# Ordering a one-core forward and backward kernel: from a greedy planner in program order to a planner by latest times with free accumulator banks

## The chip, the core and the metric

The kernel runs on one core of one Trainium2 chip. The time is device microseconds of one execution, and a kernel is judged by the median of its runs. Engines are named as the profile names them: PE (TensorE matmul) with PEld (its weight loads), DVE (VectorE), ACT (ScalarE), POOL (GpSimd), SP (SyncE). ACTq, SPq and POOLq are the queues on which these engines issue transfers.

## What is computed

The reference is a layer and its gradients. With x of 2048 rows by 512 columns:

```python
xn = layernorm(x)                               # no affine part
K  = Re( sum_n C[d,n] * exp(dt[d]*A[d,n]*l) * dt[d]*B[d,n] )   # 512 kernels of length 2048, n = 128 complex states
s  = causal_convolution(xn, K) + xn * Dskip     # the reference does it by FFTs of length 4096
g  = silu( silu(xn @ w1) @ w2 )                 # 512 -> 1792 -> 512
out = x + s * g
```

The outputs are `out` and the gradients, for a given `grad_out`, of x, the six parameter arrays of A, B and C (512 x 128 each), log_dt, Dskip, w1 and w2: twelve outputs, all bf16.

## The kernel before

Row l of x is stored as l = 16 p + t: partition p (128 of them) and t from 0 to 15. The convolution is done on four blocks of 128 channels (b = 0 to 3). Each transform is two steps of matmuls with a set of transposes between them: `dft_fwd` (tiles dA, dB; accumulators ps_s1, pt_f, ps_s2) and `dft_inv` (ps_i2, ps_i1); `cplx_mul` on DVE multiplies the spectra (tiles sp_in, cm2). The profile shortens names that end in a digit: ps_s, ps_i, ps_w.

The recorded stages are:

- Setup: x is loaded in four pieces and normalized (xn); parameters are loaded transposed by DMA (`load_params`, L609); 31 exponentials make the magnitudes (mag_all, L635); sine tables (TF, L416), small constants.
- Tables and forward (`chain`, paced with `gen_ffn_fwd` at 0.58 steps): per block `gen_tables` makes powers of the state matrix (sine on ACT, products E and Y on DVE) and, by matmuls ps_k and ps_e, the kernel KE, which goes through a DRAM tensor Kd to be read back as Kb; `gen_conv_x` transforms xn; `gen_conv_fwd` transforms Kb, multiplies and inverts. `gen_ffn_fwd` runs the two feed-forward matmuls in eight chunks of 256 rows (ps_h, hT, Silu to aT, ps_o, ob) and stores hT to Hd and ob to Od.
- Gates: `gen_gate_rows` applies Silu (g, L864) and its derivative (L873) to the feed-forward rows and forms ds and do, beside the last block's forward convolution.
- Backward convolution (`gen_conv_bwd`) beside `gen_ffn_da`, which reads Hd back (dhT), takes the derivative, multiplies by ps_da, stores DHd, and accumulates ps_dx; `gen_out` writes the forward result.
- Gradients of the state parameters (`gen_ssm_bwd`): it loads the parameters again, folds the gradient of K (GE from dKd, accumulator G, Gf), multiplies with transposed Y tables (YT, ps_v, Vb), with E (Tp) and sums on PE (psS). It runs beside the rest of `gen_ffn_da`.
- Weight gradients: `gen_dw2` (h_in transposed to a_tok, ps_w2) and `gen_dw1` (dh_tok by DMA transposes from DHd, ps_w1), then the layer norm backward `gen_ln_bwd`.

Accumulator memory has eight banks in three pools: `pf` (three tiles of one bank; feed-forward, PE transposes and weight gradients), `pc` (two tiles of two banks; transforms, ps_v, G) and `pt` (one tile of one bank; tables, psS). Evacuations go through the helper `Evac`, so L295 (ACT) and L296 (DVE) are the line of nearly all copies out of accumulators.

What sets the order is a planner at the end of the kernel. The program is written with generators that are woven by hand-set rates (`woven`, `paced`, `interleave`); that gives the recorded order. The class `Plan` then reads the recorded instructions, works out for each the instructions it must follow, and `solve` simulates the engines: every engine, SP's and POOL's queue too, takes whenever it is free the ready instruction that comes first in the recorded order. Costs come from formulas in `cost`: a matmul takes its columns at 2.4 per ns (twice that in stretches its clock model calls cold), an ACT instruction 78 ns + 0.82 per element, a change of activation table 1283 ns more; a transfer has an issue time on its queue, then 900 ns, then its packets on one shared line, then 1200 ns until a reader may start. `apply` ties each engine's instructions together in the planned order with dependencies that need no semaphore.

Two of its rules matter here:

```python
before[t.name] = first[same[-1]] if same and str(t.space) != "DRAM" else None
if len(same) >= bufs and str(t.space) != "DRAM":
    old[t.name] = users[same[-bufs]]
...
heapq.heappush(ready[eng[n]], n)
```

A tile of a tag may not start before the tile recorded ahead of it, and it waits for the users of the tile `bufs` places earlier: tiles take their buffers in turn. This holds for accumulator tiles as for others. The last line is the priority: the number n in the recorded order.

Of the kernel before, what the change touches and what calls it, by code (L numbers as in the profile page):

```python
# [18 lines left out]
P = 128  # L19
# [14 lines left out]

class Plan:
# [3 lines left out]
    SEM, ROOM = 80.0, 212863  # L39

    def __init__(self, nc, tc):
        self.tc, self.ins, self.deps, self.starts = tc, [], [], []
        cells, users, first, tags, pools, before, old, placed = {}, {}, {}, {}, {}, {}, {}, []
# [3 lines left out]
        for x in nc.cur_bb.bb.instructions:  # L47
# [16 lines left out]
            n, eng, dep = len(self.ins), x.engine.name, set()  # L64
# [4 lines left out]
            for ap, writes in [(a, False) for a in ins] + [(a, True) for a in outs]:  # L69
                t = ap.tensor  # L70
                tag = getattr(t, "tag", None)
                if tag is None:
                    if not writes:
                        continue
                elif t.name not in users:
                    same = tags.setdefault(tag, [])
                    bufs = t.tag_meta.bufs
                    before[t.name] = first[same[-1]] if same and str(t.space) != "DRAM" else None
                    if len(same) >= bufs and str(t.space) != "DRAM":
                        old[t.name] = users[same[-bufs]]  # L80
                    same.append(t.name)
                    first[t.name], users[t.name] = n, set()
                if tag is not None:
                    dep |= old.get(t.name, set())
                    if before[t.name] is not None and before[t.name] != n:
                        self.starts.append((before[t.name], n))
                    users[t.name].add(n)
                    pools.setdefault(int(tag.rsplit("_", 1)[1]), set()).add(n)
                q, idx, size = self.cells(ap)
                last, readers = cells.setdefault(t.name, (np.full(size, -1, np.int32), {}))  # L90
                spots.append((writes, q, idx, last, readers))
                for k in q:
                    for r in [last] + (list(readers.values()) if writes else []):
                        dep.update(np.unique(r[k, idx]).tolist())
            for writes, q, idx, last, readers in spots:
                for k in q:
                    if writes:
                        last[k, idx] = n
                        for r in readers.values():
                            r[k, idx] = -1  # L100
                    else:
                        readers.setdefault(eng, np.full(last.shape, -1, np.int32))[k, idx] = n
            self.deps.append(dep - {-1, n})
        for i, (a, a0, a1) in enumerate(placed):
            for b, b0, b1 in placed[i + 1:]:
                if a0 < b1 and b0 < a1 and a in pools and b in pools:
                    self.starts.append((pools[a], pools[b]))

    @staticmethod
    def cells(ap):  # L110
# [14 lines left out]
        for s, n in sorted(dims, key=lambda d: -d[0]):  # L125
            if s and n > 1:
                step = np.append(np.arange(0, n, g), n - 1) if s == 1 else np.arange(n) * s
                idx = (idx[:, None] + step).ravel()
                if s < g:
                    idx = np.unique(idx // g) * g  # L130
# [9 lines left out]
    def cost(self, x):  # L140
# [44 lines left out]
    def solve(self):  # L185

        N = len(self.ins)
        succ, wait = [[] for _ in range(N)], [len(d) for d in self.deps]
        for n, d in enumerate(self.deps):
            for m in d:  # L190
                succ[m].append(n)
        begun = [[] for _ in range(N)]
        groups = []
        for a, b in self.starts:
            if isinstance(a, int):
                begun[a].append(b)
                wait[b] += 1
            else:
                groups.append([len(a), b])
                for m in a:  # L200
                    begun[m].append(-len(groups))
                for m in b:
                    wait[m] += 1
        cost = [self.cost(x) for x in self.ins]
        eng = [x.engine.name for x in self.ins]
        dma = ["DMA" in type(x).__name__ or "Dma" in type(x).__name__ for x in self.ins]
        ready = {e: [] for e in set(eng)}
        free = dict.fromkeys(ready, 0.0)
        line, tables = 0.0, "nesd"
        heat, warm = {}, {0: False}  # L210
        self.plan = {e: [] for e in ready}
        events, self.start = [], [0.0] * N
        for n in range(N):
            if not wait[n]:
                events.append((0.0, 1, n))
        heapq.heapify(events)
        when = [0.0] * N
        end = 0.0

        def met(m, t):  # L220
            wait[m] -= 1
            when[m] = max(when[m], t)
            if not wait[m]:
                heapq.heappush(events, (when[m], 1, m))

        def clock(t):
# [3 lines left out]
            return warm[w]  # L230
        while events:
            t, kind, n = heapq.heappop(events)
            if kind == 1:
                heapq.heappush(ready[eng[n]], n)
                e = eng[n]
            else:
                e = n
            while ready[e] and free[e] <= t:
                n = heapq.heappop(ready[e])
# [6 lines left out]
                elif e == "Activation" and not dma[n]:  # L246
                    f = self.SETS.get(getattr(self.ins[n], "func", None))
                    if f:
                        both = "".join(c for c in f if c in tables)
                        if not both:  # L250
                            d, l = d + 1283.0, l + 1283.0
                        tables = both or f[0]
                self.plan[e].append(n)
                self.start[n] = t
                free[e] = t + d
                heapq.heappush(events, (free[e], 2, e))
                if dma[n]:
                    line = max(line, t + (d if e == "Pool" else min(d, 330.0)) + 900.0) + l
                    done = line + 1200.0
                else:  # L260
                    done = t + l + self.SEM
                end = max(end, done)
                for m in succ[n]:
                    met(m, t + d if e == "PE" == eng[m] else done)
                for m in begun[n]:
                    if m >= 0:
                        met(m, t)
                    else:
                        g = groups[-m - 1]
                        g[0] -= 1  # L270
                        if not g[0]:
                            for y in g[1]:
                                met(y, t)
        assert sum(map(len, self.plan.values())) == N, "the plan is not complete"
        return end

    def apply(self):

        edge = mybir.DependencyInfo(mybir.DependencyClass.NoSync, mybir.DependencyReason.DATA)
        for line in self.plan.values():  # L280
            for a, b in zip(line, line[1:]):
                self.tc.add_manual_dep(self.ins[b], self.ins[a].name, edge, reason="plan")
# [90 lines left out]
def turned_in_place(k, W, ev):  # L373

    blocks = W[:].rearrange("p a (b n) -> p (a b) n", n=P)
    turned(k, lambda i: blocks[:, i], blocks.shape[1], blocks, ev)
# [285 lines left out]
def gen_tables(k, b):  # L662
# [69 lines left out]
    bc = lambda ap, n: ap.unsqueeze(2).to_broadcast([P, ap.shape[1], n, 32])  # L732
# [4 lines left out]
    ev(KE[:, 1:8, 0:2, :], bc(A[:, 0:7], 2))  # L737
# [10 lines left out]
    ev(KE[:, 2:4, 3:6, :], bc(B[:, 3:5], 3))  # L748
    ev(KE[:, 2:8, 6:8, :], bc(B[:, 6:12], 2))
# [48 lines left out]
def gen_ffn_fwd(k):  # L798
    nc, fp = k.nc, k.fp
    D, FT, DK, T = k.D, k.FT, k.DK, k.T  # L800
    for c in range(T // 2):
# [21 lines left out]
        if c == T // 2 - 1:  # L823
            turned_in_place(k, k.W1, k.evw)
# [467 lines left out]
@with_exitstack  # L1292
def kernel(ctx, tc, A_u, A_A_re, A_A_im, A_B_re, A_B_im, A_C_re, A_C_im, A_log_dt, A_Dskip, B_x, B_w1, B_w2, grad_out,
           out_0, out_1, out_2, out_3, out_4, out_5, out_6, out_7, out_8, out_9, out_10, out_11):
    nc = tc.nc
    k = KCtx()
    k.nc, k.tc = nc, tc
    k.outs = [out_0, out_1, out_2, out_3, out_4, out_5, out_6, out_7, out_8, out_9, out_10, out_11]
    L, D, F = A_u.shape[1], A_u.shape[2], B_w1.shape[1]
# [5 lines left out]
    k.x_v, k.g_v, k.o0_v, k.o1_v = tl(A_u[0]), tl(grad_out[0]), tl(out_0[0]), tl(out_1[0])  # L1305

    def pool(name, side=None, es=ctx, **kw):
        kw.setdefault("bufs", 1)
        return es.enter_context(tc.tile_pool(name=name, side=side, reuse_waits="tile", **kw))
    dr = ctx.enter_context(tc.tile_pool(name="dram", bufs=1, space=DRAM))  # L1310
# [16 lines left out]
    k.pf = ctx.enter_context(tc.tile_pool(name="pf", bufs=3, space=PSUM))  # L1327
    k.pc = ctx.enter_context(tc.tile_pool(name="pc", bufs=2, space=PSUM))
    k.pt = ctx.enter_context(tc.tile_pool(name="pt", bufs=1, space=PSUM))
# [87 lines left out]
    turned_in_place(k, k.W2, k.evw)  # L1417
# [18 lines left out]
    plan = Plan(nc, tc)  # L1436
    plan.solve()
    plan.apply()
# [28 lines left out]
```

## Time and profile before

| | |
|---|---|
| median of three runs | 699.57 us (696.84 to 700.85) |
| profiled execution: span, first to last instruction | 694.4 us |
| profiled execution: its own total time | not given beside the span; the median above is 5.2 us more |
| instructions | 15206 |
| mean granted clock of PE | 0.950 |
| DMA | 148.85 MB, mean 214 GB/s |
| chain that ended last, by engine | PE 48%, ACT 20%, DVE 13%, DMA 9%, issue 4%, SPq 4%, ACTq 2% |
| activation table loads | nine of 1.28 us, five of them in the gates |

Busy time of an engine is the time in which one of its instructions runs; PE's overlaps PEld's. In a row for a stretch the columns are length, busy time and count of PE, PEld, DVE, ACT and POOL, then granted clock (1.00 is full), share of the 16 DMA engines and GB/s. A row of waits reads: who, its tile and line, the one waited for; total us, times, longest. A row of a timeline reads: start, duration, engine or queue, line, operation, output <- input, count.

### The profile page before, as it was taken

To read this page: it belongs to the slowest core of one execution; us is meant where nothing else is said; L and a number is where in the kernel's file an instruction comes from. 1 tells how busy PE (TensorE), PEld (TensorE's weight loads), DVE (VectorE), ACT (ScalarE), POOL (GpSimd) and SP (SyncE) were. 2 spreads that over 40 slices of the span, in tenths; PEclk is the share of its full clock that TensorE was granted. 3 is DMA by queue.
4 is the path that set the end of the run, shared out by engine and by line. 5 is a ranking of instruction groups with operands and counts; after the bars stand their busy time and mean duration, and the time that the engine had idled before them with its cause. 6 is when DMAs were issued, how large, how long until landed. Compare 5 with 4: busy or idle time off the path is not lost.

```text
span 694.4 us, 15206 instructions
## 1 busy us (share of the span) xinstructions
PE 573.5 (83%) x6268; PEld 416.6 (60%) x6268; DVE 521.0 (75%) x917; ACT 470.8 (68%) x630; POOL 79.9 (12%) x163
## 2 busy tenths in 40 slices
PE   0599697878979785469998998928998879999988
PEld 0455564547657564256765756626966656865877
DVE  6959987979989585869797979415798533966971
ACT  6959765978887988997867775406648438744541
POOL 1274100010001000000000000000002020023211
PEclk9989998999999998779999999978999999999999
DMA  9864536584557487968886775594899996747994
GB/s 297 331 145 154 196 142 225 206 274 168 189 192 260 178 292 259 287 227 274 263 273 204 236 228 176 144 236 116 168 215 221 223 252 147 172 124 243 261 253 124
DMA packets 158773, 148.85 MB, mean 214 GB/s; under 512 B 79280, under 2 KB 136112, under 8 KB 155120
## 3 DMA queue, kind: packets, MB, share of 16 engines
q1 hardware_dynamic: 145664, 125.07, 63.0%
q0 software_dynamic: 6144, 17.83, 7.1%
q10 hardware_dynamic: 6896, 4.98, 2.3%
q8 instruction: 49, 0.80, 0.5%
q14 instruction: 20, 0.16, 0.1%
HBM read 65.14 MB, written 64.36 MB: 187 GB/s over the span
## 4 chain that ended last, share of the span: by engine, by line
PE 48%; ACT 20%; DVE 13%; DMA 9%; issue 4%; SPq 4%; ACTq 2%; DVEq 0%
PE ps_w L1234 6%; PE ps_o L829 6%; PE ps_dx L1184 5%; PE ps_w L1216 5%; PE ps_da L1173 4%; ACT dA L295 4%; PE ps_h L812 2%; ACT mag_all L635 2%; PE psS L1032 2%; PE ps_i L573 2%; ACT sn L684 2%; PE pt_t L362 2%; PE ps_v L1010 2%; PE ps_i L582 2%; PE psS L1036 2%
## 5 line engine op out<-in xcount | busy, mean ns | idle before, releaser
L295 ACT CAST dA<-ps_s 128x1024 bf16<-128x1024 f32 x96 | 94.0, 1032 | 14.5 <-PE ps_s L541 9.9
L829 PE MATMUL ps_o<-W,aT 128*128 128x512 bf16 x224 | 62.8, 417 | 11.9 <-ACT hT L295 11.6
L812 PE MATMUL ps_h<-XT,W 128*128 128x256 bf16 x448 | 60.3, 279 | 6.5 <-DVE XT L296 5.0
L1173 PE MATMUL ps_da<-doT,W 128*128 128x256 bf16 x448 | 60.9, 276 | 3.1 <-ACT doT L295 1.8
L1020 DVE TENSOR_TENSOR Tp<-Vb,Eb 128x1344 bf16<-128x1344 bf16 x64 | 52.6, 855 | 10.2 <-ACT Vb L295 7.8
L1175 DVE TENSOR_TENSOR dhT<-ps_da,dhT 128x512 bf16<-128x512 f32 x56 | 37.7, 686 | 28.7 <-PE ps_da L1173 28.5
L295 ACT CAST dB<-ps_i 128x1024 bf16<-128x1024 f32 x48 | 47.0, 1027 | 17.3 <-PE ps_i L573 14.2
L295 ACT CAST Vb<-ps_v 128x672 bf16<-128x672 f32 x64 | 44.0, 740 | 18.8 <-PE ps_v L1010 15.2
L1184 PE MATMUL ps_dx<-W,dhT 128*128 128x512 bf16 x224 | 55.5, 380 | 0.0
L1216 PE MATMUL ps_w<-YD,a_tok 128*128 128x512 bf16 x224 | 53.4, 379 | 0.5 <-ACT a_tok L1201 0.5
L812 PEld LDWEIGHTS <-W 128*128 128x128 bf16 x448 | 42.4, 100 | 18.4 <-issue 10.9
L295 ACT CAST o<-ps_w 128x256 bf16<-128x256 f32 (+1 forms) x42 | 18.7, 445 | 50.0 <-PE ps_w L1234 28.1
L1234 PE MATMUL ps_w<-dh_tok,xn 128*128 128x256 bf16 x448 | 49.4, 273 | 3.1 <-DMA dh_tok<-DHd 3.1
L1173 PEld LDWEIGHTS <-W 128*128 128x128 bf16 x448 | 41.3, 99 | 13.4 <-issue 6.2
L1234 PEld LDWEIGHTS <-xn 128*128 128x128 bf16 x448 | 43.7, 98 | 8.9 <-DMA dh_tok<-DHd 2.1
L829 PEld LDWEIGHTS <-aT 128*128 128x128 bf16 x224 | 21.2, 105 | 37.9 <-issue 17.9
L573 PE MATMUL ps_i<-I,sp_in 64*128 64x128 bf16 x768 | 32.5, 229 | 11.6 <-DVE sp_in L596 8.7
L573 PEld LDWEIGHTS <-sp_in 64*128 64x128 bf16 x768 | 23.8, 99 | 24.5 <-DVE sp_in L596 12.3
L295 ACT CAST hT<-ps_h 128x512 bf16<-128x512 f32 x56 | 32.1, 617 | 8.1 <-PE ps_h L812 4.9
L296 DVE COPY dB<-pt_f 128x2048 bf16<-128x2048 bf16 x24 | 28.3, 1218 | 11.4 <-PE pt_f L547 11.4
L557 PE MATMUL ps_s<-dB,F 128*64 128x512 bf16 x192 | 29.5, 389 | 7.1 <-ACT dA L295 5.3
L295 ACT CAST pd_s<-ps_dx 128x512 bf16<-128x512 f32 x16 | 9.4, 590 | 35.7 <-DMA Pd<-pd_s 17.0
(222 smaller groups left out, 1301.9 us busy)
## 6 DMA issues: line engine op xcount, KB each, us to landing
Yd<-YD SPq DMA_DIRECT2D x8, 1024.0 KB, 5.3
sp_in<-Ud SPq DMA_DIRECT2D x8, 1024.0 KB, 8.1
h_in<-Hd SPq DMA_DIRECT2D x14, 512.0 KB, 4.8
Ed<-E SPq DMA_DIRECT2D x8, 672.0 KB, 4.0
Eb<-Ed SPq DMA_DIRECT2D x8, 672.0 KB, 5.6
Hd<-hT POOLq DMA_DIRECT2D x8, 512.0 KB, 5.8
Ud<-dA SPq DMA_DIRECT2D x4, 1024.0 KB, 4.8
KXd<-dA SPq DMA_DIRECT2D x4, 1024.0 KB, 6.0
```

The costliest lines, as they stand in the source:

```text
L295: return self.nc.scalar.copy(out=out, in_=in_)
L296: return self.nc.vector.tensor_copy(out=out, in_=in_)
L557: nc.tensor.matmul(out=ps[64 * h:64 * h + 64, 4 * v:4 * v + 4], lhsT=k.F2[:, c, :], rhs=Bv[:, u, v, h], start=True, stop=True)
L573: nc.tensor.matmul(out=ps[:, h, g], lhsT=Y[hs, c, 4 * q + g, :], rhs=k.I2[hs, c].rearrange("p c m -> p (c m)"), start=(c == 0), stop=(c == 1))
L812: nc.tensor.matmul(out=ps[:, j], lhsT=k.W1[:, dk, ft * P:ft * P + P], rhs=XTv[:, :, dk, :], start=(dk == 0), stop=(dk == DK - 1))
L829: nc.tensor.matmul(out=ps[:], lhsT=aT[:, ft, t * P:t * P + P], rhs=k.W2[:, ft, :], start=(ft == 0), stop=(ft == FT - 1))
L1020: k.nc.vector.tensor_tensor(out=Tp[:, c, :, r ^ c].rearrange("p e (q w) a -> p q w e a", w=2), in0=Vb[:, :, c].rearrange("p q w (e a) -> p ...
L1173: nc.tensor.matmul(out=ps[:, j], lhsT=k.W2[:, ft, dk * P:dk * P + P], rhs=dTv[:, :, dk, :], start=(dk == 0), stop=(dk == DK - 1))
L1175: nc.vector.tensor_tensor(out=dh[:, i0:i0 + 2, :], in0=ps[:], in1=dh[:, i0:i0 + 2, :], op=ALU.mult)
L1184: nc.tensor.matmul(out=ps[:], lhsT=dhs[ft // 8][:, ft % 8, t * P:t * P + P], rhs=k.W1[:, :, ft * P:ft * P + P], start=(ft == 0), stop=(ft ...
L1216: nc.tensor.matmul(out=ps[:], lhsT=at[:, t, :], rhs=k.do[:, t, :], start=(t == 0), stop=(t == k.T - 1))
L1234: nc.tensor.matmul(out=ps[:], lhsT=k.xn[:, t, dk * P:dk * P + P], rhs=dh[:, t].rearrange("p j n -> p (j n)"), start=(t == 0), stop=(t == k ...
```

## The change

The kernel's body becomes a function `body` that is called with a `Recorder` in the place of the engines. The recorder notes each operation with its arguments; `Room` and `Later` stand for pools and tiles, `View` for a slice of one. The noted program is then written twice by `emit`: once, in the recorded order, into a draft program from which `Plan` reads instructions and dependencies, and once into the real program, in the planner's order and with the planner's places for accumulator tiles. `tie` (formerly `apply`) ties each engine's line as before.

The planner changes in these ways:

- Accumulator tiles no longer take their buffers in turn. Each bank (or pair, in `pc`) is a place of its own; a tile takes any vacant place of its pool when its first instruction starts. The last vacant place is kept for the tile of that pool that is oldest in recorded order. Tiles in SBUF still go in turn.
- `backward` runs the plan from the end and gives every instruction the latest time at which it could start. `forward` takes, on each engine, the ready instruction with the earliest latest time, not the first recorded. The two alternate for up to eight rounds, for six settings, and the plan with the shortest modelled end is kept.
- A transfer isn't issued earlier than `hold` (30, 40 or 55 us) before its latest time.
- When the next ACT instruction would change the activation table, another that doesn't is taken first if its due time lies within `table` (3 or 8 us).
- Readers of a piece of a tile are all kept for the dependencies of the next writer, where before only the last reader of each engine was.

The costs are the same. The core of the diff:

```diff
 class Plan:
-    SEM, ROOM = 80.0, 212863
+    SEM, ROOM, LAND = 80.0, 212863, 1200.0
+    TRIES = [(hold, table) for hold in (4e4, 3e4, 5.5e4) for table in (3000.0, 8000.0)]
+    ROUNDS = 8
...
+        for (tag, bufs, space), names in tags.items():
+            lists = [list(users[t]) for t in names]
+            if space == "PSUM":
+                self.homes[tag] = bufs
+                for title, u in zip(names, lists):
+                    for n in u:
+                        self.uses[n].append(len(self.tiles))
+                    self.tiles.append((tag, u))
+                    self.titles.append(title)
+                continue
+            for a, b in zip(lists, lists[1:]):
+                if a[0] != b[0]:
+                    self.order.append(([a[0]], [b[0]]))
+            for a, b in zip(lists, lists[bufs:]):
+                for n in b:
+                    self.pred[n].update(m for m in a if m != n)
...
-    def solve(self):
+    def forward(self, key, latest=None, hold=0.0, table=0.0):
...
+        def release(n, t):
+            push(events, (max(t, latest[n] - hold) if latest and dma[n] else t, 1, n))
...
+        def full(i):
+            h = tiles[i][0]
+            q = queue[h]
+            while q and q[-1] in prior:
+                q.pop()
+            return not vacant[h] or (len(vacant[h]) == 1 and q[-1] != i)
...
-                heapq.heappush(ready[eng[n]], n)
+                push(ready[e], (key[n], n))
...
+                shut = [i for i in homeless(n) if full(i)]
+                if shut:
+                    blocked[tiles[shut[0]][0]].append(n)
+                    continue
+                if e == "Activation" and loads(n):
+                    aside, other = [], None
+                    while ready[e] and ready[e][0][0] < k + table and other is None:
...
+                for i in homeless(n):
+                    h = tiles[i][0]
+                    prior[i], slot[i] = vacant[h].pop(0)
+                    wake(h, t)
...
+    def backward(self, p):
...
+                for m in pred[n]:
+                    lag = self.LAND if dma[m] else cost[m][0] if e == "PE" == eng[m] else cost[m][1] + self.SEM
+                    need[m] = max(need[m], back[n] + lag)
...
+    def solve(self):
+
+        self.best = None
+        first = self.forward(range(self.N))
+        for hold, table in self.TRIES:
+            p = first
+            for _ in range(self.ROUNDS):
+                back = self.backward(p)
+                length = max(back)
+                p = self.forward([length - b for b in back], [p.end - b for b in back], hold, table)
+                if self.best is None or p.end < self.best.end:
+                    self.best = p
+        return self.best.end
+
+    def places(self):
+        return {self.titles[i]: ("%s_%d" % (self.tiles[i][0].rsplit("_", 2)[0], y), 1) for i, y in self.best.slot.items()}
...
+def tile_recurrent_scan__ssm_conv_s4__dense_activation_silu__prompt_kernel(ctx, tc, *args):
+    rec = Recorder()
+    ports = [View(None, None) for _ in args]
+    L, D, F = args[0].shape[1], args[0].shape[2], args[10].shape[1]
+    with ExitStack() as es:
+        body(es, rec, L, D, F, *ports)
...
+    ins, made = rec.emit(dtc, zip(ports, copies))
+    plan = Plan(draft, dtc)
     plan.solve()
-    plan.apply()
+    slots = {t.name: s for s, t in made.items() if isinstance(s, Later)}
+    order = plan.best.sequence
+    done, _ = rec.emit(tc, zip(ports, args), order, {slots[t]: home for t, home in plan.places().items()})
+    plan.tie(tc, dict(zip(order, done)))
```

More of the change, by code (lines that the diff above doesn't have):

```diff
@@ L233, in solve @@
+        loads = lambda n: self.func[n] and not dma[n] and not any(c in tables for c in self.func[n])
+        homeless = lambda n: [i for i in uses[n] if i not in prior]
+        for n in range(N):
+            if not wait[n]:
+                release(n, 0.0)
+        while events:
+            t, kind, n = pop(events)
+            if kind == 0:
+                vacate(n, t)
+                continue
+            e = n
             if kind == 1:
-                heapq.heappush(ready[eng[n]], n)
```

410 lines of the change are left out of this document (290 added, 120 removed).

## The prediction

> **What bounds the kernel now.** I read the page's busy line first, then its stretches by stage, then who waited for whom, and last the SyncE queue in the one stretch that stands still. The first two lines show busy time and granted clock.
>
> ```profile
> PE 573.5 (83%) x6268; PEld 416.6 (60%) x6268; DVE 521.0 (75%) x917; ACT 470.8 (68%) x630; POOL 79.9 (12%) x163
> ...
> PEclk9989998999999998779999999978999999999999
> ```
>
> No engine is full. Whether TensorE's 573.5 us is real work I check by rates: 32 matmuls of 512 columns in one unbroken run take 6.91 us (0.216 each), 128 of 256 columns 14.13 us (0.110), 32 transposes of 128 columns 1.79 us (0.056). 672 x 0.216 + 1344 x 0.110 + 2350 x 0.056 is 425 us; the narrow ones at their own rows' rates (L557 0.155, L573 0.039, L718 0.048, L1010 0.093, others 10 in all) add 119. So about 540 us of the 573.5 is work, and a perfect order of this work could not go below some 560 (540, plus the 20 before the first matmul). That is a floor, not a forecast.
>
> The second view is the span in stages:
>
> ```profile
> 0.00:20.00 20.00, 0.00 (x0) 0.00 (x0) 14.76 (x43) 14.27 (x26) 4.01 (x49) 1.00 0.95 297
> 20.00:104.00 84.00, 69.73 (x637) 48.79 (x638) 72.99 (x135) 64.74 (x89) 26.01 (x31) 0.94 0.55 190
> 104.00:260.00 156.00, 130.54 (x1567) 90.42 (x1566) 134.64 (x184) 125.65 (x178) 11.55 (x14) 0.97 0.62 220
> 260.00:312.00 52.00, 29.43 (x343) 23.43 (x341) 34.48 (x50) 48.63 (x49) 0.56 (x1) 0.77 0.80 258
> 312.00:441.00 129.00, 123.91 (x1511) 84.55 (x1509) 111.01 (x154) 91.36 (x102) 6.48 (x12) 0.99 0.72 229
> 441.00:471.00 30.00, 15.37 (x113) 10.48 (x111) 7.34 (x13) 6.04 (x6) 0.00 (x0) 0.84 0.84 211
> 471.00:590.00 119.00, 107.19 (x1177) 83.04 (x1174) 75.97 (x149) 71.73 (x102) 10.69 (x20) 0.95 0.89 192
> 590.00:660.00 70.00, 69.20 (x679) 51.33 (x680) 55.78 (x162) 37.87 (x62) 15.39 (x28) 1.00 0.73 199
> 660.00:694.40 34.40, 28.14 (x255) 24.51 (x253) 13.99 (x31) 10.56 (x23) 5.17 (x8) 0.99 0.79 189
> ```
>
> After the length stand busy PE, weight loads, DVE, ACT and POOL, then clock, DMA share and GB/s. The reader is to see different limits: to 260 DVE leads at 207.6 of 240 with nothing full; from 260 to 312 ACT leads (48.6 of 52); 441 to 471 nothing works; from 312 on otherwise PE is 90 to 99% busy, and an order can give little.
>
> The third view is what ended TensorE's waits:
>
> ```profile
> PE G L977 <- DMA dhT<-Hd: 14.1, 1, 14.1
> PE ps_o L829 <- ACT hT L295: 11.6, 5, 4.1
> PE ps_i L573 <- DVE sp_in L596: 8.7, 4, 4.0
> PE pt_t L362 <- ACT W L295: 5.9, 2, 5.6
> PE ps_s L557 <- ACT dA L295: 5.3, 8, 2.0
> ```
>
> Lines 2 and 4 are waits for a bank: ps_o doesn't read hT, and the transpose doesn't read the W copy before it; each waits until ScalarE has emptied the bank that its turn gives it. Line 3 is a wait for data, which no bank choice removes.
>
> The fourth is the SyncE queue in the dead stretch:
>
> ```profile
> 441.65 1.69 SPq L609 DMA_TRANSPOSE par_Ar<-in_A_A_re_dram  x1
> ...
> 448.60 1.26 SPq L609 DMA_TRANSPOSE par_Ci<-in_A_C_im_dram  x1
> ...
> 454.63 3.97 SPq L999 DMA_TRANSPOSE YT<-Yd  x2
> 458.71 0.53 SPq L1178 DMA_DIRECT2D DHd<-dhT  x1
> ...
> 461.63 0.60 SPq L961 DMA_DIRECT2D GE<-dKd  x1
> 466.61 0.38 SPq L1149 DMA_DIRECT2D dhT<-Hd  x1
> 467.04 0.59 SPq L961 DMA_DIRECT2D GE<-dKd  x1
> ```
>
> Six parameter loads, recorded first, hold the queue for 8.2 us, then four Y transposes; the GE pieces that the fold's matmul needs come last. The parameters' first reader is small DVE work (g_dBr at 447.6) for gradients that also need a finished sum.
>
> **The change, part by part.**
>
> *Recording layer and draft.* No instruction is added or removed: 6268 matmuls, 917 DVE and 630 ACT instructions stay. Cost 0; nothing runs on the chip for it.
>
> *Order by latest times.* The stall at 441 to 471: the parameter loads have late due times and fall behind GE and dhT. 14.1 us of waiting is there; 8.2 belongs to the parameter loads and the four transposes (6.6 us) may partly follow GE, so I take -11 (ends 0 and -14). What is late next is the store-then-load pair DHd, dhT (6.6 + 3.4 us on the chain). Moved past the parameters are GE, YT, Eb, DHd, Pd and dhT, all on SyncE; POOL and ACT issue none of these.
> From 20 to 260 the DVE is idle 32.4 us. 14.4 us of all DVE waits are E behind the sine, which lies on the table path that due times put first. PE's bank waits fall mostly here (next part). Together I take half of 32.4, -16 (ends 0 and -27, as the table path also has latencies that no order hides).
> From 312 to 441 PE idles 5.1: -2 (0 to -4). From 471 to 590, 11.8: -4 (0 to -8), because DMA is 0.89 busy and 3.3 us of it is the wait for YT. From 590 to 660: 0. From 660 on 6.3 us is idle, 3.1 of it for the dh_tok transposes issued at 661 to 679 behind other loads: -2.5 (0 to -4).
>
> *Banks in any order.* Bank waits on PE in the listed rows are 11.6 + 5.9, with 5.3 and 4.0 on dA partly so, 27 at most; they are counted inside the stages, not again. A gap that closes exposes DVE next (86% busy to 260). The planner keeps the last free bank for the oldest tile, so this could cost in places; the lower bound of zero gain stands in the ranges.
>
> *Table loads and the gate stretch.* From 260 to 312 ACT is the limit, with five table loads of 1.28 us alternating Silu and its derivative. Grouping saves two or three, 3 us; ACT's 3.4 idle and gate rows started earlier give the rest: -8 (0 to -14). If ACT gains a load instead, it costs 1.28.
>
> *Held loads.* A transfer may not start earlier than 30 to 55 us before its latest start. Landings are 3 to 8 us, so the hold alone costs 0; hidden by prefetch of two buffers as now. What is not covered: the planner counts 0.9 + 1.2 us around the data. For h_in that makes 3.6 us against a 4.8 median row, for dhT 3.9 against 5.0, so 1.2 short per load. Orders by due time leave the chain no margin; I charge six late loads, +7 (0 to +60, below). A late load blocks what is queued behind it on the waiting engine, and on SyncE the store behind it.
> The page "DMA: Bandwidth & Descriptors" of the Trainium skill (Latency and other measured facts) puts the memory's access at 0.2 us on average and 2 us at high load. By that the shortfall would be 1.8 us where DMA is full, an estimate from the page, six loads 11, and the result 667. The rows show 6.6 us for a DHd store in the dead stretch against its 3.9 median, which leans that way.
>
> *Written in planned order.* Waits are placed along the new order; the same pairs of engines wait. 0 (within 3 either way, the size of one such late wait).
>
> Sum: -11 - 16 - 2 - 4 - 2.5 - 8 + 7 = -36.5, on the span of 694.4: 658. The page gives the span; the median of the runs is 699.57, 5.2 more, which I add: **663**.
>
> **The rivals.**
>
> *Nearly all gaps close.* All lower ends (14 + 27 + 4 + 8 + 4 + 14 = 71) and two late loads give 694.4 - 69 + 5.2 = 631. For it: no engine is over 83%. Against: DVE at 86% to 260 with a chain that alternates four engines.
> The page "Perfetto Trace Analysis" of the Trainium skill (Identifying the Most-Contended Engine) calls matmul busy time a poor measure and points to weight-load busy time. By its measure 416.6 us, PE would have room to spare and this rival would be the forecast. The runs of matmuls above say 540 us of work, so the trace doesn't bear it out here.
>
> *Waits were latency, not order.* Only the stall (-11) and the tail (-2.5) go; 686, up to no change where late loads eat that. For it: the ps_i wait for sp_in, and ACT waiting for short PE groups (Xr 16.9, dB 14.2 us). Against: the bank waits, which are not data.
>
> *Late loads outweigh it (slower).* The place is SyncE's queue after 441 and the loads h_in, dh_tok, YT, GE, dhT: 100 and more transfers with two or three buffers each. At 1.2 us, 36 late ones cancel the 43.5 us of gains; 50 give 60 - 43.5 = +16, 716. For it: 9% of the present chain is DMA, and DMA is 0.8 to 0.9 busy from there. Against: the present order has the same costs in its planner and only one stall over 10 us.
>
> **How the numbers follow.** About 0.5% (3.5 us) is what a measurement can tell from no change. Forecast 0.46, own range 645 to 680; nearly all gaps 0.13; latency 0.16, of which 0.05 within 0.5%; slower 0.25. Hence faster 0.70, same 0.05, slower 0.25. The range runs from 634, just inside the second case, to 712, most of the slower one; outside lie about 0.07 below and 0.12 above.
>
> **What would show it.** Right: instruction counts and busy sums within 2%; the parameter transposes behind GE and G's wait under 4 us; ps_o's waits for hT under 5 us; DVE above 90% until the gates, which begin before 250; fewer than five table loads in the gates. Wrong: single PE waits over 5 us on DMA that are not there now, a busy sum that grows (contention), or PE as full as now to 260 with the same waits under other names. The likeliest error is that stages shift load so that the gain before 312 comes back as DMA waits after 441.

## The result, and the profile after

The changed kernel takes **654.77 us** (median, 653.92 to 658.25) against 699.12 for the kernel before in the same measurement: a ratio of **0.9377, 95% interval 0.9338 to 0.9416**. The forecast was 663.0 with a range of 634 to 712. The profiled execution has a span of 652.2 us (before 694.4) and a mean granted clock of 0.976 (before 0.950). Two of the runs below had one execution that took over 1.5% more than their fastest, and their ratios and times leave it out.

In the changed kernel every instruction carries the line of `emit`, L144, so it is read by tiles. The chain of work that ended last reaches back only over a quarter of the span, so I read stretches. First the busy line and the clock of the page:

```profile
PE 568.0 (87%) x6268; PEld 414.4 (64%) x6268; DVE 525.7 (81%) x917; ACT 469.0 (72%) x630; POOL 86.5 (13%) x163
...
PEclk9988999979999999979999999999989999999999
```

The work is the same: PE, DVE and ACT are within 1% of their old sums; POOL's, a small one, is 6.6 us (8%) longer. The 42.2 us are mostly idle time that was closed: PE's idle time falls from 121 to 84 us, its busy time by 5.5. Now the stretches, cut where the same work begins and ends (start of gates, first ps_da, last du_b, G at its height). The columns after the length are busy PE, weight loads, DVE, ACT, POOL, then clock, DMA share, GB/s:

```profile
20.00:237.00 217.00, 187.74 (x2087) 132.83 (x2088) 206.55 (x302) 182.95 (x265) 41.53 (x43) 0.97 0.68 236
237.00:291.00 54.00, 38.06 (x466) 29.71 (x462) 38.44 (x55) 53.91 (x56) 1.40 (x2) 0.87 0.75 255
291.00:416.00 125.00, 120.27 (x1477) 81.76 (x1474) 107.16 (x152) 91.40 (x101) 5.42 (x10) 1.00 0.68 220
416.00:470.00 54.00, 48.69 (x421) 34.55 (x419) 27.65 (x39) 21.13 (x28) 1.08 (x2) 1.00 0.93 208
470.00:590.00 120.00, 111.34 (x1308) 86.60 (x1309) 90.58 (x223) 76.67 (x112) 20.48 (x38) 0.99 0.95 208
590.00:652.20 62.20, 59.02 (x499) 46.62 (x497) 37.04 (x96) 28.44 (x51) 10.82 (x18) 0.99 0.86 230
```

Until the gates DVE is busy 206.6 of 217 us (before, between the same times, 186.3); in the gates ACT is full (53.9 of 54); from 291 on PE is 90 to 96% busy, the old dead stretch included. By the starts of the same instructions in both traces:

| stretch | before | after | difference | predicted |
|---|---|---|---|---|
| start to first ps_da | 310.0 | 290.5 | -19.5 | -16 - 8 = -24 |
| first ps_da to last du_b | 129.9 | 125.5 | -4.4 | -2 |
| last du_b to the end | 254.5 | 236.2 | -18.3 | -11 - 4 - 2.5 + 7 = -10.5 |
| sum | 694.4 | 652.2 | -42.2 | -36.5 |

What ended PE's waits is now small, and the 14.1 us of G is 1.6:

```profile
PE pt_t L144 <- DVE xn L144: 15.2, 1, 15.2
PE ps_i L144 <- ACT dB L144: 9.7, 6, 2.7
PE ps_h L144 <- ACT hT L144: 5.6, 7, 1.5
PE ps_i L144 <- DVE sp_in L144: 4.4, 2, 4.1
...
PE G L144 <- DMA GE<-dKd: 1.6, 1, 1.6
...
PE ps_o L144 <- ACT hT L144: 0.6, 1, 0.6
```

xn and sp_in are waits for data, and so are 5.3 of the 9.7 us for dB. The waits for a bank behind hT's copy have not all gone: ps_o's fell from 11.6 to 0.6 us, but ps_h's, which reads no hT either, grew from 1.4 to 5.6. Together they fell from 13.0 to 6.2.

The SyncE queue where the dead stretch was (start, duration, queue, line, operation, tile):

```profile
417.95 0.70 SPq L144 DMA_DIRECT2D GE<-dKd  x1
418.70 6.48 SPq L144 DMA_TRANSPOSE YT<-Yd  x4
425.23 0.59 SPq L144 DMA_DIRECT2D GE<-dKd  x1
...
433.05 1.19 SPq L144 DMA_TRANSPOSE par_Bi<-in_A_B_im_dram  x1
434.29 1.45 SPq L144 DMA_TRANSPOSE par_Cr<-in_A_C_re_dram  x1
435.79 0.60 SPq L144 DMA_DIRECT2D GE<-dKd  x1
...
442.88 1.85 SPq L144 DMA_TRANSPOSE par_Ai<-in_A_A_im_dram  x1
444.83 0.53 SPq L144 DMA_DIRECT2D Pd<-pd_s  x1
445.41 0.60 SPq L144 DMA_DIRECT2D GE<-dKd  x1
```

G's first product needs four GE pieces. Two of them now lead the parameter loads, but the third stands among them and the fourth (445.41) behind all six, and G's first product with GE starts 34.3 us after the last du_b starts (before: 30.9). The stall wasn't removed; it was filled. From 416 to 460 PE is busy 40.2 of 44 us, with ps_da and ps_dx, whose last matmul starts at 461.0 where it started at 514.3.

### The profile page after: what moved, and what is told of

The parts are those of the page before. It is cut to its first block, busy times and chain, and to the rows that moved or that the text cites. A ratio compares the mean times of both kernels' runs of the same rounds, so it can differ in the third digit from the quotient of the medians.

```text
span 652.2 us, 15213 instructions
## 1 busy us (share of the span) xinstructions
PE 568.0 (87%) x6268; PEld 414.4 (64%) x6268; DVE 525.7 (81%) x917; ACT 469.0 (72%) x630; POOL 86.5 (13%) x163
## 5 line engine op out<-in xcount | busy, mean ns | idle before, releaser
L144 PEld LDWEIGHTS <-W 128*128 128x128 bf16 x1008 | 91.0, 99 | 45.1 <-issue 29.2
L144 ACT CAST dA<-ps_s 128x1024 bf16<-128x1024 f32 x96 | 96.7, 1029 | 22.4 <-PE ps_s L144 18.2
L144 PE MATMUL ps_h<-XT,W 128*128 128x256 bf16 x448 | 61.2, 281 | 9.6 <-ACT hT L144 5.6
L144 PE MATMUL ps_da<-doT,W 128*128 128x256 bf16 x448 | 60.8, 273 | 5.0 <-DVE dhT L144 3.4
L144 PE MATMUL ps_o<-W,aT 128*128 128x512 bf16 x224 | 58.9, 394 | 4.3 <-ACT aT L144 3.7
L144 PEld LDWEIGHTS <-xn 128*128 128x128 bf16 x512 | 48.2, 99 | 22.0 <-DVE xn L144 15.2
L144 DVE TENSOR_TENSOR Tp<-Vb,Eb 128x1344 bf16<-128x1344 bf16 x64 | 51.4, 849 | 11.8 <-ACT Vb L144 11.8
L144 PE MATMUL ps_dx<-W,dhT 128*128 128x512 bf16 x224 | 57.8, 380 | 0.5 <-DVE dhT L144 0.5
L144 ACT CAST dB<-ps_i 128x1024 bf16<-128x1024 f32 x48 | 47.6, 1024 | 14.1 <-PE ps_i L144 13.8
L144 PE MATMUL ps_w<-YD,a_tok 128*128 128x512 bf16 x224 | 55.1, 379 | 0.9 <-ACT o L144 0.9
L144 DVE TENSOR_TENSOR dhT<-ps_da,dhT 128x512 bf16<-128x512 f32 x56 | 38.1, 687 | 21.0 <-PE ps_da L144 19.5
L144 ACT CAST Vb<-ps_v 128x672 bf16<-128x672 f32 x64 | 44.4, 734 | 11.9 <-PE ps_v L144 8.3
L144 PE MATMUL ps_w<-dh_tok,xn 128*128 128x256 bf16 x448 | 51.3, 273 | 0.0
L144 ACT CAST o<-ps_w 128x256 bf16<-128x256 f32 (+1 forms) x42 | 18.3, 443 | 40.8 <-PE ps_w L144 36.2
L144 PE MATMUL psS<-Tp,ident 128*128 128x128 bf16 (+1 forms) x688 | 45.1, 220 | 1.4 <-DVE Tp L144 1.3
L144 PEld LDWEIGHTS <-ident 128*128 128x128 bf16 x688 | 41.1, 99 | 4.6 <-DVE Tp L144 2.1
L144 PE MATMUL ps_i<-I,sp_in 64*128 64x128 bf16 x768 | 32.6, 225 | 11.3 <-DVE sp_in L144 4.4
L144 DVE TENSOR_TENSOR cm<-sp_in,dA 128x1024 bf16<-128x1024 bf16 x48 | 30.9, 685 | 12.6 <-ACT dA L144 6.0
L144 PEld LDWEIGHTS <-sp_in 64*128 64x128 bf16 x768 | 24.0, 98 | 23.9 <-issue 13.2
L144 ACT CAST hT<-ps_h 128x512 bf16<-128x512 f32 x56 | 32.0, 602 | 7.7 <-PE ps_i L144 3.1
L144 PEld LDWEIGHTS <-aT 128*128 128x128 bf16 x224 | 20.5, 101 | 25.3 <-issue 5.0
L144 PE MATMUL ps_s<-dB,F 128*64 128x512 bf16 x192 | 30.4, 394 | 5.8 <-DVE dB L144 4.1
```

Of the source, the lines that this page charges most:

```text
L144: getattr(getattr(nc, engine), op)(*[on(a) for a in args], **{w: on(a) for w, a in kw.items()})
```

## Experiments

Theory: the gain comes from order, with banks counted inside it, and the stall at 441 goes because the parameter loads move behind GE. Each run was measured beside the kernel before, whose median moved between 696.35 and 701.29 us from one measurement to the next, so ratios compare between runs and microseconds only roughly. Rivals: free banks make the gain; the stall was worth nothing by itself; a part that was priced at zero (held loads, written order) carries it; late loads take something back.

### Banks alone

```diff
     def solve(self):
         self.best = None
         first = self.forward(range(self.N))
+        self.best = first
+        return first.end
```

The priority stays the recorded order; accumulator tiles take any bank.

> The changed program with the recorded order as priority (the first forward pass alone): accumulator tiles take any vacant bank, nothing else of the planner's change is left. Theory A (the order by latest times carries most of the 44 us, the banks about 11): 699 - 11 = 688, range 680 to 697. Theory B (the bank turns were what held the engines, the order adds little): most of the gain is here already, 660 to 672. If ps_o's waits for hT are still over 8 us although any bank may be taken, those waits were not for a bank.

Measured: 711.93 us, ratio 1.0237 (1.0181 to 1.0293): slower by 1.8 to 2.9%, which neither theory had. The reason lies in pf's three banks. The tiles that transpose W1 and W2 for the backward pass are ready at once:

```profile
13.26 1.89 PE L144 MATMUL pt_t<-ident,W 128*128 128x128 bf16 x16 [13.26 <-DMA W<-in_B_w_dram]
...
261.41 1.01 ACT L144 COPY W<-pt_t 128x1024 bf16<-128x1024 bf16 x1 [1.11 <-PE ps_h L144]
...
272.54 0.69 DVE L144 COPY W<-pt_t 128x1024 bf16<-128x1024 bf16 x1 [10.51 <-PE ps_h L144]
```

Two of them (16 transposes) take two of three banks at 13 us. Their copies must wait until the feed-forward pass has read the weights they overwrite, so the banks come free at 261 and 273 us. The pass runs on one bank: PE's ps_h waits 12.6 us for hT's copy (before 1.4). The next run tests this alone.

```diff
+                for z, (title, u) in enumerate(zip(names, lists)):
+                    reads = [y.bass_ap.tensor.name for y in self.ins[u[0]].ins if getattr(y, "bass_ap", None) is not None]
+                    if z and "pt_t" in title and any("W1" in y or "W2" in y for y in reads):
+                        self.order.append(([lists[z - 1][0]], [u[0]]))
```

In addition to the edit above, a W transpose may not begin before the tile recorded ahead of it.

> The run with vacant banks and recorded order as priority again, but a tile that turns a weight matrix (pt_t from W1 or W2) may not start before the tile recorded just ahead of it; all other tiles still take any vacant bank. In the run without this, two such tiles were written at 13.3 us, could be copied out only at 261 and 272, when the forward feed-forward no longer needed the weights, and so held two of pf's three banks for 250 us; the first ps_da came at 328.8 against 310.0. Theory H (these held banks are the whole loss): the loss of 15 us goes and the 11 us that I had given to free banks shows, 685 to 692, with ps_da at or before 310. Rival (free banks under the recorded order lose for other reasons, as any tile may run ahead and hold a bank): 702 or more, ps_da after 318.

Measured: 702.49 us, ratio 1.003 (0.9994 to 1.0065). The loss is gone, so those two tiles were its cause; the expected gain (685 to 692) doesn't show in its place, and the first ps_da still starts at 317.8 (before 310.0). Free banks without a new order are worth about nothing here. ps_o's waits for hT's copy are still 8.2 us (before 11.6) although it may take any bank, so most of that wait was not owed to the turn.

### Order alone

```diff
-            if space == "PSUM":
+            if space == "none":
```

Accumulator tiles keep their turn; the order is by latest times.

> Order by latest times, holds and table rule as changed, but accumulator tiles take their buffers in turn, in recorded order, as before the change. Theory A: 665 (10 us above the changed kernel's 655), range 658 to 675. Theory B: 685 or more, because without free banks the due times cannot be kept. If the parts do not add up (both this and the run with banks alone are slow), each needs the other.

Measured: 681.85 us, ratio 0.9794 (0.9748 to 0.984), between the two theories. It *loses* 15 us up to the first ps_da (325.2, before 310.0) and gains 30 behind it. Its stretch to 237 us:

```profile
20.00:237.00 217.00, 167.09 (x1825) 119.54 (x1838) 198.19 (x295) 164.84 (x230) 31.73 (x38) 0.91 0.59 207
```

PE does 20.7 us less there than in the changed kernel's line for the same stretch. So the parts don't add: banks +2.4%, order -2.1%, together -6.2%. I read it so: an order by latest times wants urgent tiles to pass others, which a turn forbids; which banks matter is tested next but one.

The same plan, with the real program written in the recorded order and only tied to the plan:

```diff
-    done, _ = rec.emit(tc, zip(ports, args), order, {slots[t]: home for t, home in plan.places().items()})
-    plan.tie(tc, dict(zip(order, done)))
+    done, _ = rec.emit(tc, zip(ports, args))
+    plan.tie(tc, done)
```

> The same plan as the run with latest times and banks in turn (order by latest times, buffers in turn), but the program is written in the recorded order and only tied into the planned one, as the kernel before does it. Theory: writing the program in the planned order costs and brings nothing, so within 3 us of that run. Rival: the place of the writing decides which waits are inserted, and the recorded order leaves stale waits: 5 us or more slower than that run.

Measured: 684.95 us (678.28 to 688.31), ratio 0.9813 (0.9736 to 0.989), beside 0.9794: no difference shows. The interval leaves room for some 5 us either way, so the 3 us that were expected are not told from nothing.

Which banks have to be free? Only pf's three, in the changed kernel:

```diff
-            if space == "PSUM":
+            if space == "PSUM" and tag.startswith("pf"):
```

> The changed kernel, ordered by latest times, with only the three banks of pf in any order (transposes of weights, the FFN forward and backward, the weight gradients). The tiles of pc (scan, convolution, fold: two banks) and pt (ps_k, psS: one) keep their recorded turn. All in turn gave 0.979 of the kernel before, all free 0.938. Theory A (the gain is from pf: the weight gradients of dw1 and the W transposes share it with the FFN, and in turn the dh_tok matmuls can't start before 621 us): 652 to 660 us, ps_w from dh_tok starts before 530, the forward convolution ends (S_b) by 290. Theory B (pc's and pt's turn holds up the scan and the fold as well): 664 to 680, dh_tok matmuls start early all the same, but S_b ends at 293 or later and G's last matmul after 550. Theory C (pf makes no difference without the others): 680 to 690.

Measured: 655.19 us, ratio 0.9411 (0.9381 to 0.9441), which overlaps the whole change's. The first theory holds. Up to 237 us its row is the changed kernel's again:

```profile
20.00:237.00 217.00, 184.60 (x2063) 131.60 (x2080) 203.66 (x300) 182.71 (x266) 42.28 (x43) 0.98 0.68 236
```

The first ps_da starts at 290.1 and the dw1 matmuls (ps_w from dh_tok) at 539.2 (under 530 was expected); in turn they started at 325.2 and 621.0. In turn, the feed-forward pass ends later too (last ps_o at 296.1, here 270.4), and so do the W transposes (280.7 to 314.4; in the changed kernel 217.0 to 270.7). Which of pf's tiles held up which in the first 290 us wasn't isolated.

### The stall

In the kernel before, the parameter loads are recorded later: first at step 2 of the loop in `gen_ssm_bwd` (L1102 and following), then at step 5 (`i == 5`).

```diff
-    par = load_params(k, sb, 0, k.D)
-    par["dt"] = k.dt[:]
+    par = {}
...
+        if i == 2:
+            par.update(load_params(k, sb, 0, k.D))
+            par["dt"] = k.dt[:]
```

> The kernel before, with the six parameter loads of the state gradients recorded two groups later, so that GE, YT and Eb come ahead of them on SyncE; nothing else differs. Theory S (SyncE's order made the stall of 441 to 471): TensorE's 14 us wait at G falls under 5 and the time to 688 to 692. Rival P (TensorE stood behind G although other matmuls could have run, and GE is late anyway because of the Y transposes and the DHd store): the wait at G stays over 8 us and the time within 4 us of 699.

Measured: 700.61 us, ratio 1.0053 (1.0023 to 1.0084), as the rival had it. The wait at G stays, 14.7 us: the loads were moved behind two GE pieces, and the fourth piece (462.13) still stands behind all six.

> The kernel before, with the six parameter loads recorded five groups later, just ahead of the first gradient that reads them, so that not only GE but also the DHd stores and dhT loads of the feed-forward backward come ahead of them on SyncE. Theory S (the parameters' 8 us on SyncE make the stall, by way of dhT and DHd as much as GE): G's wait under 6 us, 689 to 694. Rival P (SyncE is full there with Y transposes and the rest anyway, and TensorE's fixed order puts G ahead of the matmuls that could run): wait at G over 9 us, 697 to 701.

Measured: 700.38 us, ratio 1.0008 (0.9969 to 1.0047). This time PE's wait is gone, and the time is still that of the rival, which had expected the wait to stay. PE's waits from 430 to 520 us in this run:

```profile
PE pt_t L362 <- ACT pd_s L295: 5.8, 1, 5.8
PE G L977 <- issue: 2.2, 2, 1.9
PE ps_da L1175 <- DVE dhT L1177: 0.7, 1, 0.7
```

But G doesn't begin earlier: 472.6 (before 470.8). The SyncE queue shows why:

```profile
444.10 0.70 SPq L961 DMA_DIRECT2D GE<-dKd  x1
...
450.69 0.61 SPq L961 DMA_DIRECT2D GE<-dKd  x1
...
456.75 1.48 SPq L609 DMA_TRANSPOSE par_Ar<-in_A_A_re_dram  x1
...
463.55 0.60 SPq L961 DMA_DIRECT2D GE<-dKd  x1
...
465.52 1.26 SPq L609 DMA_TRANSPOSE par_Ci<-in_A_C_im_dram  x1
...
468.04 1.34 SPq L961 DMA_DIRECT2D GE<-dKd  x1
```

Only two GE pieces lead the parameters here as well. The planner keeps the pieces apart: each writes every fourth partition of GE, its map of a tile (`cells`) knows only blocks of 32 partitions, so it takes each piece to overwrite the one before and puts it behind that one's landing (3.5 us, the median before). Other loads fill the queue in between. In the kernel before there is one more link, in this row of SyncE's waits: a load of dhT waits for a DHd store, and the last GE piece stands behind it:

```profile
SPq L1149 <- DMA DHd<-dhT: 4.3, 1, 4.3
```

So no run has all four GE pieces ahead of the parameters, and what an earlier G would be worth stays open. What params_last shows is that PE's wait of 14 us was worth nothing by itself: PE is busy 80.4 us between 430 and 520 (before 73.7), but 2.9 us less between 520 and 600; after 520 it waits 5.5 us for h_in (before 1.2), and the last psS starts at 618.1 (before 618.4).

### Held loads

```diff
-    TRIES = [(hold, table) for hold in (4e4, 3e4, 5.5e4) for table in (3000.0, 8000.0)]
+    TRIES = [(hold, table) for hold in (1e9,) for table in (3000.0, 8000.0)]
```

A transfer may be issued as soon as its data and place are there.

> The changed kernel without the hold: a transfer may be issued as soon as it is ready. My prediction gave the hold nothing: within 4 us of 655. Rival: holding back loads that nobody needs yet is what keeps SyncE and the DMA engines free for the urgent ones; then 663 or more, with longer waits on DMA between 415 and 480.

Measured: 673.48 us, ratio 0.9586 (0.9513 to 0.9658). The first 290 us are the changed kernel's (first ps_da 289.2), and G begins 2.5 us later; all the rest of the 21.5 us that the profiled execution is longer comes after that. SyncE's queue between 465 and 512 us, the dh_tok loads alone:

```profile
470.61 5.64 SPq L144 DMA_TRANSPOSE dh_tok<-DHd  x1
479.94 5.41 SPq L144 DMA_TRANSPOSE dh_tok<-DHd  x1
486.12 2.46 SPq L144 DMA_TRANSPOSE dh_tok<-DHd  x1
492.44 4.69 SPq L144 DMA_TRANSPOSE dh_tok<-DHd  x1
497.81 5.30 SPq L144 DMA_TRANSPOSE dh_tok<-DHd  x1
506.52 4.21 SPq L144 DMA_TRANSPOSE dh_tok<-DHd  x1
```

They take 27.7 of 47 us on the queue that also issues YT, GE and Eb; the changed kernel issues two (10.4 us). DVE's largest wait from 460 to 600 us, without hold:

```profile
DVE Tp L144 <- ACT Vb L144: 30.9, 8, 7.7
```

and with it:

```profile
DVE Tp L144 <- ACT Vb L144: 11.8, 5, 4.2
```

Vb comes from ps_v, whose matmuls and weight loads wait 9.8 us for YT over the whole kernel (with the hold 3.7), while YT's transfers, once issued, land in a median of 4.8 us (5.1). So YT was late in being issued, not in landing. G's last matmul starts at 571.1 against 541.9. To see whether it is these loads, the next run holds them alone:

```diff
+        self.tok = [d and any("dh_tok" in y for y in named(x)) for d, x in zip(self.dma, self.ins)]
...
-            push(events, (max(t, latest[n] - hold) if latest and dma[n] else t, 1, n))
+            push(events, (max(t, latest[n] - hold) if latest and self.tok[n] else t, 1, n))
```

> The changed kernel, but only the transposing loads of dh_tok are held back to 30 to 55 us before their latest start; every other transfer may be issued as soon as its data and its place are there. It separates what the hold is worth for. Theory A (dh_tok loads of up to 5.6 us each, taken early on SyncE, delay YT, GE and Eb between 470 and 512 us): the time is that of the changed kernel within 5 us (650 to 660), G's last matmul ends near 542 and DVE's wait of Tp for ScalarE's Vb between 460 and 600 us is near 12 us. Theory B (the hold matters for the early weight loads and the loads of the forward stages as well): the time stands between the two, 664 to 674, and the first 290 us look as in the kernel without hold. Theory C (any load taken early is as bad): 671 to 676, as without hold.

Measured: 654.48 us, ratio 0.9387 (0.9322 to 0.9452): all of it comes back, and G's last matmul starts at 540.7. Its two loads in that stretch and its wait for Vb:

```profile
499.69 3.98 SPq L144 DMA_TRANSPOSE dh_tok<-DHd  x1
505.08 3.80 SPq L144 DMA_TRANSPOSE dh_tok<-DHd  x1
```

```profile
DVE Tp L144 <- ACT Vb L144: 14.6, 8, 4.7
```

The hold is worth 2.1% (0.9586 against 0.9377; about 15 us, with the intervals some 9 to 20), and fourteen transfers make it. Some of it may be the choice of plans, two settings without the hold against six, which wasn't separated. The planner's `cost` books 2.46 us of SyncE's time for each; in the changed kernel they take a median of 3.8.

### Smaller terms, and a try at a faster version

The rule that takes another ACT instruction before one that loads a table, switched off:

```diff
-    TRIES = [(hold, table) for hold in (4e4, 3e4, 5.5e4) for table in (3000.0, 8000.0)]
+    TRIES = [(hold, table) for hold in (4e4, 3e4, 5.5e4) for table in (0.0,)]
```

> The changed kernel without the rule that passes over an instruction which would change ACT's table. The prediction gave grouped table loads about 3 us: 656 to 660, with eleven or more table loads where the changed kernel has nine. Rival: due times group them by themselves, same count and within 2 us of 655.

Measured: 662.34 us, ratio 0.9445 (0.9383 to 0.9507), with eleven table loads instead of nine. The intervals overlap; two loads are 2.6 us, and the rest isn't told apart.

The planner's landing allowance doubled, and then also the W tiles held back as above:

```diff
-    SEM, ROOM, LAND = 80.0, 212863, 1200.0
+    SEM, ROOM, LAND = 80.0, 212863, 2400.0
```

> The changed kernel with the planner's allowance for the landing of a transfer doubled, from 1.2 to 2.4 us, nothing else. My prediction charged 7 us for loads that the planner orders 1.2 us too late. If that term is real, the time falls by 4 to 8 us (647 to 651) and the DMA waits on TensorE and VectorE shrink. If late loads cost nothing here (TensorE's DMA waits in the dead stretch of before are 1.6 and 1.7 us in the changed kernel), the time moves only as far as another order by the same planner does, within 4 us of the changed kernel either way, and no wait for a transfer changes by more than 3 us.

> The changed kernel with both: the tiles of the transposed W1 and W2 may not begin before the tile before them in the recorded order, so that they can't take a free bank early, and an allowance of 2.4 us for a landing. It is the candidate for a faster version. With banks alone, holding these tiles back brought 9.4 us, because two of them sat on two of three banks from 13 to 272 us. Theory A (ordering by latest times already keeps these tiles from starting early: the first W transpose of the changed kernel starts at 217 us): no gain from this part, the time is that of the run with the allowance alone within 4 us. Theory B (they still hold banks that the stages before 290 us want): 4 to 8 us less than that run, with ps_o's last matmul before 252 us.

Measured: 652.16 us (648.66 to 653.05), ratio 0.9312 (0.9263 to 0.9362), and 662.64 us, ratio 0.9469 (0.9433 to 0.9506). The first overlaps the changed kernel's interval: perhaps some 4 us faster, not shown; its profile shows the longest of its four executions, so no waits are compared. The second is about 11 us slower than the first, against both theories: a constraint that brought some 2% in one order (1.0237 to 1.003) cost 1.6% in another. Why is open; its first ps_da is 3.8 us later than the changed kernel's and its last psS 9.1 us. (The 9.4 us in its expectation compare medians of two measurements; by the ratios that gain was about 14.)

## Why the prediction was right, and where it wasn't

The total was 8 us too high, inside the likeliest case's own range. Of the 8.2 us, 5.7 are in the span (-42.2 for -36.5). The other 2.6 are in the step from the span to the median: 5.2 was added, and it is 2.6 here. Every execution whose span is listed takes 1.7 to 2.2 us more than that, so the 5.2 also held a profiled execution that was faster than the median. That the total came so near is in part luck, as the last stretch gained what was forecast, and more, in another way. Step by step:

- **Order to 260 us (-16) and gates (-8): the size nearly right, -19.5 for -24.** DVE is busy 214.2 of the first 220 us and the gates begin at 236.6, as named. But the gates then take longer (first g to first ps_da 53.9 us, before 45.7), with ACT full and the end of the feed-forward pass now among them (last ps_o at 255.3; before at 262.7, ahead of the first g): the two terms were not separable. The table count was wrong: three loads stand in the gates where five did, but two more stand ahead of them, nine as before. Grouping saved nothing in ACT's total; its gain in the gates was paid earlier.
- **Banks counted inside the stages: right as a sum, wrong as a picture.** I took them as 17.5 to 27 us of waits that go, each a wait for the bank that the turn gives. With any bank free, 8.2 of ps_o's 11.6 us were still there under the recorded order. Alone, free banks cost 2.4% or nothing, and pf's three make 35 us of difference before the first ps_da, with the order. I had even priced the mechanism of the loss ("could cost in places") without a place; the run gave it one.
- **The stall (-11): the failed step.** "The parameter loads have late due times and fall behind GE and dhT": they fell behind two of the four GE pieces that G needs, the fourth still follows all six, and G begins no earlier after du_b (34.3 us, before 30.9). I had read the GE pieces as coming last because the parameters were recorded first; the planner ties each piece to the landing of the one before. The stretch behind du_b did gain 18.3 us (-17.5 predicted without late loads), by other work in the gap: ps_da and ps_dx 53 us earlier, and dw1's matmuls from 517.7 instead of 638.7 on. That the sum still fits is luck. The trace said what ended the wait at G; it did not say that the end depended on it, and in params_last the wait goes and no time with it.
- **Held loads (0): wrong by about 15 us.** I costed the hold as a price (is a load late?) and not as a benefit (what does an early load delay?). Without it the stretch behind du_b is 258.8 us in the profiled execution, the longest of four, and 254.5 before: the whole gain of that stretch hangs on the hold.
- **Six late loads (+7): not seen.** PE, DVE and ACT wait for DMA 43.6 us in all (before 63.8); PE's longest in the dead stretch's place are 1.6 and 1.2. The term is nearly as large as what the forecast was high by, but the other terms erred too, and the doubled allowance doesn't exclude 4 us of it. The slower rival, which needed 36 late loads, stays out.
- **Written order (0): not contradicted**, 0.9813 beside 0.9794.
- **Nearly all gaps close (631): not reached.** The page "Perfetto Trace Analysis" of the Trainium skill (Identifying the Most-Contended Engine) has it that matmul busy time is no good measure of how near a kernel is to its limit, and names the achieved FLOP rate (MFU) and weight-load busy time instead; MFU isn't worked out here. Of the two busy times, that of matmuls was the better guide. Before, the stretch from the first ps_da to the last du_b and the one behind it had weight loads 65% and 67% of the time, but matmuls 96% and 87%, and they gained 3.4% and 7.2%.

## What to carry to other kernels

A wait of one engine, however long, is worth what ends earlier when it goes; try it alone before counting it, and see in the trace that the trial moved what it was to move. A planner orders by the dependencies that it believes in: read those before blaming the priorities. Free choice of a buffer paid here only together with an order that keeps unneeded work from starting: ready-but-not-urgent tiles and transfers otherwise took the banks and the queue first. In a sum, ask of every rule that delays something what it lets pass, and not only what it makes late.

## What the runs showed of the hardware

A transposing load cost its issuing queue far more here than a plain one: the fourteen dh_tok loads of the changed kernel, of 512 KB each, hold SyncE 2.0 to 6.0 us (median 3.8), the sixteen plain loads of dhT (512 and 384 KB) 0.36 to 1.55 us (median 0.37). To landing it is 6.9 against 4.9 us for plain loads of 512 KB (medians, not at equal load of the DMA engines). The page "Advanced Engine Details and Errata" of the Trainium skill (X-Bar Transpose (TRN2)) holds that transposing DMAs are as fast as regular ones; by these rows that isn't so for the queue. That it is the queue's time which the hold saves fits YT's late issue and unchanged landing, but no run tells the queue's time from the load on the DMA engines.
